# Softmax sums in smaller TensorE tiles, split by query halves, with a new instruction order (attention and a snake MLP on one core)

## The chip, the cores and the metric

The kernel runs on one core of a Trainium2 chip. The core has engines that each work through their own instruction queue in order: TensorE (PE: matmuls; PEld: its weight loads), VectorE (DVE), ScalarE (ACT), GpSimd (POOL) and SyncE (SP, which only issues transfers). They meet through semaphores. Operands lie in SBUF, matmul results in PSUM. The metric is the device time of the core in microseconds, from the first instruction to the last; lower is better.

## The reference

Attention with RMS-normalised queries and keys over 8 batches, 12 heads, 448 positions and head size 64, and then a two-layer product whose activation is `h + sin(alpha h)^2 / alpha`:

```python
def _attn_ref(q, k, v, g_q, g_k):          # q, k, v: (8, 12, 448, 64)
    q_n, k_n = (rmsnorm(q, g_q), rmsnorm(k, g_k))
    scores = np.matmul(q_n, k_n.transpose(0, 1, 3, 2)) / np.sqrt(q.shape[-1])
    attn = np.exp(scores - np.max(scores, axis=-1, keepdims=True))
    attn = attn / (np.sum(attn, axis=-1, keepdims=True) + 1e-09)
    return np.matmul(attn, v)

def _moe_ref(x, w_in, w_out, alpha):       # x: (3584, 768), d_ff 2048
    h = x @ w_in
    s = np.sin(alpha * h)
    g = h + s * s / (alpha + 1e-09)
    return g @ w_out
```

The rows of `x` are the positions of all batches, its columns the heads side by side. Inputs and output are float32. The kernel computes in bf16 on TensorE and leaves out the maximum before the exponential.

## The kernel before

Per batch, the 12 heads are three chunks of four heads: two head pairs `pp` by two halves `hi`. Each chunk is normalised, transposed, and multiplied to scores with the keys on the partitions, one tile of 64 keys per head at a time (seven tiles `j` make 448 keys). A score tile fills a PSUM pair of banks; ScalarE turns it into `expT`.

```python
    def scores(c, j, warm=0):

        sc = bank_pair("sc")
        for _ in range(warm):
            nc.tensor.matmul(sc[:, 0], blank[:, :P], blank, start=True, stop=True)
        for pp in range(2):
            for hi in range(2):
                qkt, r = qkT[2 * c + pp], slice(hi * 64, hi * 64 + 64)
                nc.tensor.matmul(sc[pp * 64:pp * 64 + 64, hi, :S], qkt[r, 1, j * REST:(j + 1) * REST], qkt[r, 0, :],
                                 start=True, stop=True)
        expT[c, j] = epool.tile([P, 2, S], BF16, tag="expT", name="expT")
        nc.scalar.activation(expT[c, j], sc[:, :, :S], ACT.Exp, scale=SCALE)
        give_back(sc)

    avs, recs = {}, {}
```

The sums over the keys come from a product with ones, so that each sum stands on all partitions of its head, where the product with the values stands too. `attend` does both. The first chunk of a batch ("ones 0", "values 0") uses 64x64 tiles: half `hi` of the heads on output partitions `hi * 64`, head pair `pp` in its own PSUM bank. The other two chunks together ("ones 1", and the low and high columns of the values) use 64x32 tiles in four strips of 32 partitions. Ln and Exp(-x) on ScalarE give the reciprocals `rec`, and VectorE multiplies the values with them into `xT`:

```python
    def attend(b, what, tiles=range(NJ)):

        kind, both = what.split()
        both = both == "1"
...
        last = 1 if pre else NJ - 1
        for j in tiles:
            for hi in range(2):
                for c in ((1, 2) if both else (0,)):
                    for pp in range(2):
                        r = slice(pp * 64, pp * 64 + 64)
                        o, k = (strip(c, pp, hi), c - 1) if both else (slice(hi * 64, hi * 64 + 64), pp)
                        d = slice(kind == "high", D, 2) if both and kind != "ones" else slice(D // 2 if both else D)
                        w = ones[r, d] if kind == "ones" else vb[b][r, 2 * c + hi, j, d]
                        x = pre.parts[j] if pre else expT[b * NC + c, j]
                        nc.tensor.matmul(av[o, k, :S], w, x[r, hi, :], start=(j == 0), stop=(j == last))
        if tiles[-1] < last:
            return
        if kind == "ones":
            rec = recs[both] = pre.t if pre else rpool.tile([P, 2, S], F32, tag="rec", name="rec")
            for k in ((0, 1), (1, 2)) if both and b == 0 else ((0, 2),):
                nc.scalar.activation(rec[:, slice(*k)], av[:, slice(*k), :S], ACT.Ln)
                nc.scalar.activation(rec[:, slice(*k)], rec[:, slice(*k)], ACT.Exp, scale=-1.0)
            give_back(avs.pop(what))
        else:
            if b not in xT:
                xT[b] = xpool.tile([P, KT, S], BF16, tag="xT", name="xT")
            first = 0 if not both else 2 if kind == "low" else 3
            for k in (slice(0, 1), slice(1, 2)) if both and b == 0 else (slice(0, 2),):
                kts = slice(first + k.start * (1 + both), first + (k.stop - 1) * (1 + both) + 1, 1 + both)
                nc.vector.tensor_mul(xT[b][:, kts, :], av[:, k, :S], recs[both][:, k])
            give_back(avs.pop(what))

```

(`pre` is not used by these plans: no batch adds tiles up beforehand.) Then come the first product (`hps`, 16 row tiles `m` of 128, over six row groups `kt` of the weights in the order 0, 1, 2, 4, 3, 5), the snake activation, and the second product, which is left over as filler work for the next batch's attention. Its pieces ("units") each hold a PSUM pair for 16 steps; a filler call does two steps, eight 64x64 matmuls:

```python
    def snake(b, ps, m):
        hps = ps[:, m % 2, :S]
        s1 = spool.tile([P, S], F32, tag="s1", name="s1")
        nc.scalar.activation(s1, hps, ACT.Sin, scale=alpha_sb[:, m, :])
        s2 = spool.tile([P, S], F32, tag="s2", name="s2")
        if m % 2 == 0:
            nc.gpsimd.tensor_mul(s2, s1, s1)
        else:
            nc.scalar.activation(s2, s1, ACT.Square)

        def finish():
            nc.vector.scalar_tensor_tensor(
                g_sb[:, m, (b % 2) * S:(b % 2 + 1) * S], s2, inv_alpha_sb[:, m, :], hps, op0=ALU.mult, op1=ALU.add)
            if m % 2:
                give_back(ps)
        return finish
...
                for r in range(2):
                    for o in range(2):
                        rs, os = slice(r * 64, r * 64 + 64), slice(o * 64, o * 64 + 64)
                        nc.tensor.matmul(st["ps"][os, r, :HALF], g_sb[rs, m, c0 + o * 64:c0 + o * 64 + 64],
                                         w_out_sb[rs, m, half * HALF:(half + 1) * HALF], start=(m == 0), stop=(m == MT - 1))
                if m == MT - 1:
                    ...
                    nc.vector.tensor_copy(osb[:, 0], st["ps"][:, 0, :HALF])
                    nc.vector.tensor_add(osb[:, 0], osb[:, 0], st["ps"][:, 1, :HALF])
                    give_back(st["ps"])
```

The order of all this is written out as plans: one for batch 0, one for batch 1, one for batches 2 to 7. In a plan `S` is a score tile (with a number: that many warming matmuls first), a number alone is so many filler calls on the current unit, `f` one on the next unit, `o` and `v` are tiles of the first chunk's sums and values, `x`, `y`, `z` those of the other chunks' sums, low and high values. `q`, `u`, `g`, `r`, `k`, `p`, `t` are the steps of the normalisation (square, reduce, gains, reciprocal root, scale, transpose on TensorE or by DMA) of a chunk; `l`, `V`, `W`, `O` load queries and keys, values, first and second weights; `D` lets GpSimd wait for a chunk's keys. The string of digits says which of the four PSUM pairs each taker gets; the dictionary says what goes beside the first product.

Of the kernel before, what the change touches and what calls it, by code (L numbers as in the profile page):

```python
# [17 lines left out]
try:  # L18
# [7 lines left out]
AX = mybir.AxisListType  # L26
ACT = mybir.ActivationFunctionType
# [3 lines left out]

STAGE_0 = (
    (
        "q000 u000 G q010 q011 u010 q001 u011 r01 u001 r00 g00 q11 q10 g01 k01 D1 k00 V00 L p012 p00 u10 "
        "V01 u11 W12 S2 S q20 r1 u20 g1 k11 l3 q21 k10 S2 l4 S S4 S W01 g2 S1 u21 p1 r2 k20 o7 S1 V02 S "
        "q30 k21 v7 u30 S S4 q31 D2 u31 S S1 W00 p2 r3 S3 g3 S S2 k31 S2 q40 D4 W02 S2 k30 q41 p3 S1 u40 "
        "W10 l5 W11 O01 q51 S x4 u41 y3 q50 S r4 z2 z2 x3 y4 g4 z1 z2 "
    ),
    "30123103213013230120310232103102310231302130213",
    {-1: 'u50 u51 g5', 1: 'k401 O00 l6', 2: 'k411', 3: 'O10', 4: 'k400', 5: 'k410', 7: 'O11', 8: 'p4 V12 l7 V10 V11'},  # L40
)
STAGE_1 = (
    (
        "2 q31 4 q40 S 2 u31 S 1 S 1 S r2 1 f q41 1 f 1 S S 1 f f k21 k20 1 S t2 2 S 2 S 1 u40 u41 1 q30 "
        "g3 S 2 f o2 u30 S r4 f 1 f 1 S 1 f o5 2 f r3 l5 2 f g4 f S 2 S 2 V11 S 1 S 2 k31 v1 k41 k30 k40 "
        "S v2 S v4 V12 S y1 S y1 S z3 x7 z3 q51 y5 l6 V10 z1 "
    ),
    "0212310313131230222101013032013001230123",
    {-1: 'l7 q50', 0: 'u51', 2: 'g5 t4', 4: 'u50', 8: 't3'},
)  # L50
STAGE_N = (
    (
        "1 r2 q31 q30 f 2 S V10 f 3 V11 f f k20 2 S 3 S 2 k21 S u31 q40 1 t2 1 g3 1 S 1 f u30 S 2 f S f S "
        "r3 q41 f f 1 l5 1 f S 4 u40 S S 5 S S u41 o7 v7 S S 5 S 2 q51 f S 2 S q50 k31 k30 2 S g4 1 u50 S "
        "2 r4 t3 1 S z3 x7 k40 y7 z1 z2 z1 "
    ),
    "01232302102020301301320321310130210231023",
    {-1: 'l6 u51 V12', 1: 'k41', 2: 't4 l7', 3: 'g5'},
)
LAST = "0123012"  # L60

# [7 lines left out]
def kernel(  # L69
# [23 lines left out]
    nc = tc.nc  # L93
    B, H, S, D = q.shape
# [8 lines left out]
    NJ = S // REST  # L103
    assert P == 2 * REST == 2 * D
    NC = NP // 2
# [28 lines left out]
    def bank_pair(name, dtype=F32):  # L134
        slot = int(upcoming.popleft())
        free_at.remove(slot)
        ps = psum.tile([P, 2, 2048 // mybir.dt.size(dtype)], dtype, tag=f"ps{slot}", name=name)
        slot_of[id(ps)] = slot
        return ps

    def give_back(ps):
        free_at.append(slot_of.pop(id(ps)))
# [3 lines left out]
    def strip(c, pp, hi):  # L146

        s = 2 * hi + (pp if c == 1 else 1 - pp)
        return slice(s * 32, s * 32 + 32)

    def load_qk(ci, k_queue=nc.sync):

        b, dp = ci // NC, ci % NC
        qk[ci] = inp.tile([P, 2, 2 * NJ, D], F32, tag="qk", name="qk")
        for which, src, queue in ((0, q, nc.sync), (1, k, k_queue)):
            heads = src[b].rearrange("(dp hi pp) (p j) d -> dp pp p hi (j d)", hi=2, pp=2, j=NJ)[dp]
            rows = qk[ci][:, which].rearrange("p (hi j) d -> p hi (j d)", hi=2)
            if ci == 0:
                continue
            if dp < 2:  # L160
                queue.dma_start(out=rows, in_=heads.rearrange("pp p hi x -> (pp p) hi x"))
            else:
                for pp in range(2):
                    queue.dma_start(out=rows[pp * 64:pp * 64 + 64], in_=heads[1 - pp])
        if ci == 0:
            for hi in range(2):
                for which, src, queue in ((0, q, nc.sync), (1, k, k_queue)):
                    heads = src[b].rearrange("(dp hi pp) (p j) d -> dp hi pp p (j d)", hi=2, pp=2, j=NJ)[dp, hi]
                    rows = qk[ci][:, which].rearrange("p (hi j) d -> p hi (j d)", hi=2)
                    queue.dma_start(out=rows[:, hi], in_=heads.rearrange("pp p x -> (pp p) x"))  # L170
                if hi == 0:
                    load_g()
# [17 lines left out]
    def load_g():  # L190
        for i, (src, queue) in enumerate(((g_q, nc.sync), (g_k, nc.scalar))):
            queue.dma_start(out=g_rows[:, i], in_=src.rearrange("(a d) -> a d", a=1))

    load_qk(0, nc.scalar)
    load_qk(1, nc.scalar)
    load_qk(2)
    nc.gpsimd.dma_start(out=small, in_=moe_alpha.rearrange("(mt p) -> mt p", p=P))
    nc.scalar.preload_act_table_set(EXP_LN)
# [2 lines left out]
    ones = const.tile([P, D], BF16)  # L201
# [58 lines left out]
    qkT, expT, xT = {}, {}, {}  # L260
# [125 lines left out]
# [6 lines that stand above are left out]
        if tiles[0] == 0:  # L392
            avs[what] = bank_pair("av")
        av = avs[what]
        pre = presums.get(b) if what == "ones 0" else None
        last = 1 if pre else NJ - 1
        for j in tiles:
            for hi in range(2):
                for c in ((1, 2) if both else (0,)):
                    for pp in range(2):  # L400
# [7 lines that stand above are left out]
            return  # L408
        if kind == "ones":
            rec = recs[both] = pre.t if pre else rpool.tile([P, 2, S], F32, tag="rec", name="rec")  # L410
            for k in ((0, 1), (1, 2)) if both and b == 0 else ((0, 2),):
                nc.scalar.activation(rec[:, slice(*k)], av[:, slice(*k), :S], ACT.Ln)
                nc.scalar.activation(rec[:, slice(*k)], rec[:, slice(*k)], ACT.Exp, scale=-1.0)  # L413
            give_back(avs.pop(what))
# [8 lines that stand above are left out]
# [185 lines left out]
    for b in range(B):  # L608
        plan, slots, h_plan = (STAGE_0, STAGE_1, STAGE_N)[min(b, 2)]
        if b:  # L610
            nc.scalar.preload_act_table_set(EXP_LN)
            fillers.extendleft(reversed(second_product(b - 1)))
        tiles = deque((b * NC + c, j) for c in range(NC) for j in range(NJ))
        upcoming.extend(slots)
        done = {what: 0 for what in STEPS}
        for x in tokens_of(plan):
            if x in "Ff":
                fill(x == "f")
            elif x[0] == "S":
                scores(*tiles.popleft(), int(x[1:] or 0))  # L620
            elif x[0] in STEPS:
                n = int(x[1:] or 1)
                attend(b, STEPS[x[0]], range(done[x[0]], done[x[0]] + n))
                done[x[0]] += n
            else:
                step(b, x)
        first_product(b, {i: [lambda t=t: step(b, t) for t in tasks.split()] for i, tasks in h_plan.items()})
        assert not upcoming and not tiles
# [32 lines left out]
```

## The time and profile before

The median of three runs is 417.75 us (417.33 to 418.62). The profiled execution spans 417.9 us.

| | busy us | share of the span |
|---|---|---|
| TensorE (PE) | 397.1 | 95% |
| ScalarE (ACT) | 317.4 | 76% |
| GpSimd (POOL) | 285.3 | 68% |
| VectorE (DVE) | 227.1 | 54% |

| group | count | busy us |
|---|---|---|
| first product, L449 | 768 matmuls | 146.8 |
| second product in quadrants, L528 | 3072 matmuls | 145.6 |
| exponentials, L361 | 168 | 144.9 |
| scores, L358 | 672 matmuls | 58.3 |
| sums and values, L406 | 1792 matmuls | 62.4 |

How to read it: busy times of one engine's groups overlap where matmuls of several tiles run side by side, so a group's busy time is the union of its records and not its share of the total. A matmul's own duration (349 ns for 448 columns) contains the passage through the array; the pace is read from the distance between the starts of groups. "Idle before" with a releaser says what an engine waited for. Idle time of an engine that does not set the pace costs nothing.

### The profile page before, as it was taken

How to read it: one execution, taken by the hardware profiler on the slowest of the kernel's cores; microseconds unless marked ns; L12 is line 12 of the kernel's file. 1: busy time of each engine (PE TensorE's matmuls, PEld its weight loads, DVE VectorE, ACT ScalarE, POOL GpSimd, SP SyncE). 2: the span in 40 equal slices, each digit the busy share in tenths (PEclk: the TensorE clock that was granted, in tenths of full speed). 3: DMA queues.
4: the chain of work that ended last, by engine and by line, in shares of the span. 5: the costliest groups of instructions: out<-in, count | busy, mean ns of one | idle time of the engine just before them, and what ended most of it. 6: DMA issues, size and time to landing. Idle time of an engine off the chain costs nothing.

```text
span 417.9 us, 14897 instructions
## 1 busy us (share of the span) xinstructions
PE 397.1 (95%) x6598; PEld 238.2 (57%) x6601; DVE 227.1 (54%) x339; ACT 317.4 (76%) x467; POOL 285.3 (68%) x270
## 2 busy tenths in 40 slices
PE   2797999889999999999999999999999999999996
PEld 2243558645666557655666456655576556665563
DVE  5786475426674565564575466655565464335511
ACT  4897789748889679877889688987889688886600
POOL 4999889966786879597796688597795784003300
PEclk9999999999999999999999999999999999999999
DMA  8999999798085744847374744736385521620022
GB/s 244 212 220 255 167 218 156 168 284 105 3 164 131 168 139 83 175 92 156 101 175 119 174 134 80 176 81 164 104 131 158 93 46 27 96 61 0 2 75 75
DMA packets 66788, 54.51 MB, mean 130 GB/s; under 512 B 38164, under 2 KB 62500, under 8 KB 66724
## 3 DMA queue, kind: packets, MB, share of 16 engines
q1 hardware_dynamic: 53250, 40.06, 37.8%
q0 software_dynamic: 12512, 11.81, 19.7%
q10 hardware_dynamic: 962, 1.70, 1.1%
q8 instruction: 51, 0.84, 0.8%
q14 instruction: 13, 0.11, 0.1%
HBM read 45.62 MB, written 11.01 MB: 136 GB/s over the span
## 4 chain that ended last, share of the span: by engine, by line
PE 86%; DMA 6%; POOL 4%; issue 2%; DVE 1%; ACTq 0%; SPq 0%; ACT 0%; DVEq 0%; POOLq 0%
PE hps L449 34%; PE ops L528 29%; PE av L406 11%; PE sc L358 6%; PE ops L509 5%; DMA w_in<-in_moe_w_in_dram 3%; DMA qk<-in_k_dram 2%; POOL sq L283 1%; DMA out_dram<-osb 1%; POOL qk L288 1%; POOL vb L182 0%; POOL vb L185 0%; SPq L499 0%; POOL w_in L244 0%; DVE osb L534 0%
## 5 line engine op out<-in xcount | busy, mean ns | idle before, releaser
L361 ACT ACTIVATE expT<-sc 128x896 bf16<-128x896 f32 x168 | 144.9, 914 | 16.9 <-PE sc L358 16.0
L449 PE MATMUL hps<-xT,w_in 128*128 128x448 bf16 x768 | 146.8, 353 | 2.1 <-DMA w_in<-in_moe_w_in_dram 2.1
L528 PE MATMUL ops<-w_out_sb,g_sb 64*64 64x384 bf16 x3072 | 145.6, 323 | 0.2 <-ACT expT L361 0.2
L435 DVE SCALAR_TENSOR_TENSOR g_sb<-s,inv_alpha_sb,hps 128x448 bf16<-128x448 f32 x128 | 80.8, 677 | 67.3 <-POOL s L430 66.9
L449 PEld LDWEIGHTS <-w_in 128*128 128x128 bf16 x768 | 74.4, 98 | 74.0 <-issue 3.0
L528 PEld LDWEIGHTS <-g_sb 64*64 64x64 bf16 x3072 | 91.3, 107 | 38.0 <-issue 2.7
L430 POOL TENSOR_TENSOR s<-s 128x448 f32<-128x448 f32 x64 | 59.5, 932 | 74.7 <-ACT s L427 50.2
L427 ACT ACTIVATE s<-hps,alpha_sb 128x448 f32<-128x448 f32 x128 | 74.4, 626 | 43.2 <-PE hps L449 40.4
L283 POOL TENSOR_TENSOR sq<-qk 128x896 f32<-128x896 f32 x44 | 73.3, 1682 | 26.1 <-DMA qk<-in_k_dram 21.1
L311 POOL TENSOR_TENSOR qkn<-qk,inv 128x448 bf16<-128x448 f32 x80 | 72.7, 938 | 2.5 <-ACT inv L302 2.0
L358 PE MATMUL sc<-qkT 64*64 64x448 bf16 x672 | 58.3, 356 | 3.6 <-DVE qkT L343 2.1
L534 DVE COPY osb<-ops 128x384 f32<-128x384 f32 x48 | 26.7, 557 | 51.3 <-PE ops L528 46.1
L288 POOL TENSOR_TENSOR qk<-qk,gg 128x896 f32<-128x896 f32 (+1 forms) x25 | 50.3, 2016 | 1.2 <-ACT g_sb L280 1.1
L292 DVE TENSOR_REDUCE ms<-sq 128x14 f32<-128x896 f32 x44 | 46.7, 1078 | 6.4 <-POOL sq L283 6.3
L421 DVE TENSOR_TENSOR xT<-av,rec 128x896 bf16<-128x896 f32 (+1 forms) x26 | 25.6, 1015 | 37.2 <-ACT rec L413 30.7
L406 PE MATMUL av<-expT,vb 64*32 64x448 bf16 (+1 forms) x1120 | 37.9, 350 | 2.7 <-issue 2.0
L432 ACT ACTIVATE s<-s 128x448 f32<-128x448 f32 x64 | 36.9, 577 | 3.0 <-DVE g_sb L435 0.2
L358 PEld LDWEIGHTS <-qkT 64*64 64x64 bf16 x672 | 20.7, 107 | 17.3 <-issue 7.9
L406 PEld LDWEIGHTS <-vb 64*32 64x32 bf16 (+1 forms) x1120 | 19.5, 95 | 16.7 <-issue 6.8
L535 DVE TENSOR_TENSOR osb<-osb,ops 128x384 f32<-128x384 f32 x48 | 26.6, 554 | 1.7
L406 PE MATMUL av<-expT,ones 64*32 64x448 bf16 (+1 forms) x672 | 24.5, 349 | 0.0
L509 PE MATMUL ops<-w_out_sb,g_sb 128*128 128x384 bf16 x128 | 21.0, 326 | 0.0
(46 smaller groups left out, 173.5 us busy)
## 6 DMA issues: line engine op xcount, KB each, us to landing
out_dram<-osb SPq DMA_DIRECT2D x39, 192.0 KB, 3.7
qk<-in_q_dram SPq DMA_DIRECT2D x15, 448.0 KB, 5.5
qk<-in_k_dram SPq DMA_DIRECT2D x14, 448.0 KB, 6.3
qk<-in_q_dram SPq DMA_DIRECT2D x18, 224.0 KB, 4.3
qk<-in_k_dram SPq DMA_DIRECT2D x16, 224.0 KB, 4.7
vb<-in_v_dram POOLq DMA_DIRECT2D x16, 224.0 KB, 4.4
w_out_sb<-in_moe_w_out_dram POOLq DMA_DIRECT2D x4, 768.0 KB, 7.7
out_dram<-osb SPq DMA_DIRECT2D x26, 96.0 KB, 3.4
```

Of the source, the lines that this page charges most:

```text
L283: nc.gpsimd.tensor_mul(st.sq[w], qk[ci][:, w], qk[ci][:, w])
L288: nc.gpsimd.tensor_mul(x, x, gg.to_broadcast([P, len(heads) * NJ, D]))
L292: nc.vector.reduce_sum(st.ms[:, w, rows], st.sq[w][:, rows], axis=AX.X)
L311: eng.tensor_mul(n[:, :, hi, :], x[:, hi], inv[:, hi].unsqueeze(2).to_broadcast([P, NJ, D]))
L358: nc.tensor.matmul(sc[pp * 64:pp * 64 + 64, hi, :S], qkt[r, 1, j * REST:(j + 1) * REST], qkt[r, 0, :], start=True, stop=True)
L361: nc.scalar.activation(expT[c, j], sc[:, :, :S], ACT.Exp, scale=SCALE)
L406: nc.tensor.matmul(av[o, k, :S], w, x[r, hi, :], start=(j == 0), stop=(j == last))
L427: nc.scalar.activation(s1, hps, ACT.Sin, scale=alpha_sb[:, m, :])
L430: nc.gpsimd.tensor_mul(s2, s1, s1)
L435: nc.vector.scalar_tensor_tensor(g_sb[:, m, (b % 2) * S:(b % 2 + 1) * S], s2, inv_alpha_sb[:, m, :], hps, op0=ALU.mult, op1=ALU.add)
L449: nc.tensor.matmul(ps[:, m % 2, :S], w_in_sb[m * 2 // MT][:, kt, m % (MT // 2) * P:(m % (MT // 2) + 1) * P], x[:, kt, :], start=(kt == ORD ...
L528: nc.tensor.matmul(st["ps"][os, r, :HALF], g_sb[rs, m, c0 + o * 64:c0 + o * 64 + 64], w_out_sb[rs, m, half * HALF:(half + 1) * HALF], star ...
```

## The change

For batches 1 to 7 the sums of the first chunk are no longer formed in 64x64 tiles. Each tile's 448 queries are cut in two halves `qh`, and each half is multiplied with only 32 columns of ones, so that the sums of query half `qh` of heads `hi` stand on the strip of 32 partitions `2 * hi + qh`. That makes eight 64x32 tiles of 224 columns where four 64x64 tiles of 448 columns were. It is meant to use TensorE for half as many columns. The product with the values still wants all 448 reciprocals on all 64 partitions of its head, so the missing half is brought over from the partner strip: VectorE "sums" over an axis of one element, reading 32 partitions and writing another 32. ScalarE takes Ln of half as many elements and writes Exp(-x) twice, once into the other half of the columns as the source of these moves.

The plans are all new, with the same number of score tiles, filler calls and warming matmuls (apart from one filler call of each plan that works on the current unit instead of the next). In batch 0 the sums stay as they were. The keys of the second chunk are loaded by SyncE's queue instead of ScalarE's. The diff:

```diff
--- before.py
+++ after.py
@@ -31,31 +31,31 @@
 
 STAGE_0 = (
     (
-        "q000 u000 G q010 q011 u010 q001 u011 r01 u001 r00 g00 q11 q10 g01 k01 D1 k00 V00 L p012 p00 u10 "
-        "V01 u11 W12 S2 S q20 r1 u20 g1 k11 l3 q21 k10 S2 l4 S S4 S W01 g2 S1 u21 p1 r2 k20 o7 S1 V02 S "
-        "q30 k21 v7 u30 S S4 q31 D2 u31 S S1 W00 p2 r3 S3 g3 S S2 k31 S2 q40 D4 W02 S2 k30 q41 p3 S1 u40 "
-        "W10 l5 W11 O01 q51 S x4 u41 y3 q50 S r4 z2 z2 x3 y4 g4 z1 z2 "
+        "q010 u010 G q000 q011 u011 q001 u000 r01 u001 g00 g01 r00 q10 D1 k01 k00 V02 W00 p012 q11 g1 W02 "
+        "u10 p00 q21 u11 r1 q20 k11 k10 S2 V00 g2 S1 l3 S S2 u21 S u20 S1 r2 W11 q30 L l4 p1 k20 k21 S2 "
+        "q31 S3 u30 S1 u31 S2 S S1 o1 S4 p2 r3 V01 S D2 g3 k31 W01 l5 o3 W10 o3 D4 W12 k30 S1 v7 S1 p3 "
+        "q40 q41 u40 S S2 S1 O01 q50 S1 S u41 x3 O00 y2 y4 x4 y1 z7 r4 g4 u50 q51 "
     ),
-    "30123103213013230120310232103102310231302130213",
-    {-1: 'u50 u51 g5', 1: 'k401 O00 l6', 2: 'k411', 3: 'O10', 4: 'k400', 5: 'k410', 7: 'O11', 8: 'p4 V12 l7 V10 V11'},
+    "12010210130112302302310203231023103210321032132",
+    {-1: 'O10 u51 k410 l6', 0: 'O11', 2: 'k411', 3: 'g5', 5: 'k401 k400', 6: 'V10', 8: 'p4 V12 V11 l7'},
 )
 STAGE_1 = (
     (
-        "2 q31 4 q40 S 2 u31 S 1 S 1 S r2 1 f q41 1 f 1 S S 1 f f k21 k20 1 S t2 2 S 2 S 1 u40 u41 1 q30 "
-        "g3 S 2 f o2 u30 S r4 f 1 f 1 S 1 f o5 2 f r3 l5 2 f g4 f S 2 S 2 V11 S 1 S 2 k31 v1 k41 k30 k40 "
-        "S v2 S v4 V12 S y1 S y1 S z3 x7 z3 q51 y5 l6 V10 z1 "
+        "1 q31 2 S 2 q30 2 f 2 r2 S 1 u31 S q41 2 S S 2 k20 f k21 f S t2 f 1 S u30 3 S 1 f S 1 q40 l5 g4 "
+        "1 g3 2 S f S 3 u41 1 u40 o6 V12 o1 v1 2 S 2 f r3 v4 S v2 1 k31 f S f S 1 S f 1 S 1 k30 1 t3 S "
+        "q50 2 S S z4 l6 S r4 x5 x1 z1 x1 y6 V11 y1 z1 z1 g5 k41 k40 "
     ),
-    "0212310313131230222101013032013001230123",
-    {-1: 'l7 q50', 0: 'u51', 2: 'g5 t4', 4: 'u50', 8: 't3'},
+    "0132102102023301312322121210213130123023",
+    {-1: 'l7 u50', 0: 't4 q51', 2: 'V10', 8: 'u51'},
 )
 STAGE_N = (
     (
-        "1 r2 q31 q30 f 2 S V10 f 3 V11 f f k20 2 S 3 S 2 k21 S u31 q40 1 t2 1 g3 1 S 1 f u30 S 2 f S f S "
-        "r3 q41 f f 1 l5 1 f S 4 u40 S S 5 S S u41 o7 v7 S S 5 S 2 q51 f S 2 S q50 k31 k30 2 S g4 1 u50 S "
-        "2 r4 t3 1 S z3 x7 k40 y7 z1 z2 z1 "
+        "f q40 f 1 f 2 q41 1 S 1 r2 5 f S f f S 2 S 1 u40 k20 1 k21 S 1 u41 1 S 2 S 1 q31 1 o7 1 f f 1 S "
+        "t2 f 1 r4 S 2 f 1 l5 q30 S 3 S 1 u31 1 S 2 u30 g3 V10 S 2 S S k41 3 S v6 r3 k30 S k31 v1 S 2 V12 "
+        "g4 2 S 2 S 2 q51 l6 S t3 z3 x7 y5 y2 z4 V11 "
     ),
-    "01232302102020301301320321310130210231023",
-    {-1: 'l6 u51 V12', 1: 'k41', 2: 't4 l7', 3: 'g5'},
+    "01223131310312323203013012301021310231023",
+    {-1: 'k40', 0: 't4', 2: 'q50', 3: 'u50', 4: 'u51 g5', 6: 'l7'},
 )
 LAST = "0123012"
 
@@ -192,7 +192,7 @@
             queue.dma_start(out=g_rows[:, i], in_=src.rearrange("(a d) -> a d", a=1))
 
     load_qk(0, nc.scalar)
-    load_qk(1, nc.scalar)
+    load_qk(1)
     load_qk(2)
     nc.gpsimd.dma_start(out=small, in_=moe_alpha.rearrange("(mt p) -> mt p", p=P))
     nc.scalar.preload_act_table_set(EXP_LN)
@@ -394,7 +394,16 @@
         av = avs[what]
         pre = presums.get(b) if what == "ones 0" else None
         last = 1 if pre else NJ - 1
+        halved = what == "ones 0" and b > 0
         for j in tiles:
+            if halved:
+                for hi in range(2):
+                    for qh in range(2):
+                        for pp in range(2):
+                            r, o = slice(pp * 64, pp * 64 + 64), slice((2 * hi + qh) * 32, (2 * hi + qh) * 32 + 32)
+                            nc.tensor.matmul(av[o, pp, :S // 2], ones[r, :D // 2], expT[b * NC, j][r, hi, qh * S // 2:(qh + 1) * S // 2],
+                                             start=(j == 0), stop=(j == NJ - 1))
+                continue
             for hi in range(2):
                 for c in ((1, 2) if both else (0,)):
                     for pp in range(2):
@@ -408,7 +417,16 @@
             return
         if kind == "ones":
             rec = recs[both] = pre.t if pre else rpool.tile([P, 2, S], F32, tag="rec", name="rec")
-            for k in ((0, 1), (1, 2)) if both and b == 0 else ((0, 2),):
+            if halved:
+                cols = [slice(0, S // 2), slice(S // 2, S)]
+                nc.scalar.activation(rec[:, :, cols[0]], av[:, :, cols[0]], ACT.Ln)
+                nc.scalar.activation(rec[:, :, cols[1]], rec[:, :, cols[0]], ACT.Exp, scale=-1.0)
+                nc.scalar.activation(rec[:, :, cols[0]], rec[:, :, cols[0]], ACT.Exp, scale=-1.0)
+                for hi in range(2):
+                    for qh in range(2):
+                        src, dst = (slice((2 * hi + x) * 32, (2 * hi + x) * 32 + 32) for x in (qh, 1 - qh))
+                        nc.vector.reduce_sum(rec[dst, :, cols[qh]], rec[src, :, cols[qh]].unsqueeze(3), axis=AX.X)
+            for k in () if halved else ((0, 1), (1, 2)) if both and b == 0 else ((0, 2),):
                 nc.scalar.activation(rec[:, slice(*k)], av[:, slice(*k), :S], ACT.Ln)
                 nc.scalar.activation(rec[:, slice(*k)], rec[:, slice(*k)], ACT.Exp, scale=-1.0)
             give_back(avs.pop(what))
```

## The prediction

> **What bounds the kernel now.** I read the page's busy shares first, then the busy time of each engine in windows cut where a batch's first product (line 449) starts, then TensorE's waits, then groups by line and shape, then TensorE in order of time.
>
> ```profile
> PE 397.1 (95%) x6598; PEld 238.2 (57%) x6601; DVE 227.1 (54%) x339; ACT 317.4 (76%) x467; POOL 285.3 (68%) x270
> ```
>
> ```profile
> 0.00:41.79 41.79, 28.99 (x459) 13.83 (x462) 29.62 (x51) 30.87 (x48) 34.86 (x41) 1.00 1.01 233
> 41.79:90.20 48.41, 44.82 (x805) 29.54 (x806) 23.18 (x37) 39.27 (x57) 44.87 (x45) 1.00 0.98 189
> 90.20:137.50 47.30, 47.30 (x853) 28.82 (x854) 27.76 (x41) 37.97 (x57) 32.16 (x28) 1.00 0.58 115
> 137.50:184.81 47.31, 47.31 (x855) 28.83 (x854) 27.09 (x40) 39.07 (x58) 37.35 (x34) 1.00 0.58 136
> ...
> 374.87:417.90 43.03, 39.07 (x225) 21.77 (x224) 16.18 (x23) 14.74 (x25) 7.46 (x8) 0.98 0.14 38
> ```
>
> After the length come busy PE, PEld, DVE, ACT, POOL, then the granted clock, DMA share and GB/s. There are three regimes. From 90 to 375 us TensorE is busy for all of each 47.3 us period: what leaves TensorE there leaves the total, and work on VectorE (27 of 47 us) is free unless it delays TensorE. Up to 90 us the DMA engines are full (1.01 and 0.98) and GpSimd nearly so (44.87 of 48.41); TensorE is idle 48.41 - 44.82 = 3.6 us in the second window. The last window has no attention in it.
>
> ```profile
> PE hps L449 <- DMA w_in<-in_moe_w_in_dram: 2.1, 1, 2.1
> PE av L406 <- issue: 2.0, 2, 1.6
> PE sc L358 <- DVE osb L535: 1.4, 1, 1.4
> ```
>
> The idle time that a better order could recover is small: 2.1 us for weights at 39.7 us, 1.4 us at 79 us for a PSUM pair that VectorE has not emptied, 1.6 us at 87.8 us with no releaser shown.
>
> ```profile
> L406 PE MATMUL av<-expT,ones 64*32 64x448 bf16 x448 | 12.3, 349 | 0.0
> L406 PE MATMUL av<-expT,ones 64*64 64x448 bf16 x224 | 12.2, 349 | 0.0
> L413 ACT ACTIVATE rec<-rec 128x448 f32<-128x448 f32 x2 | 1.2, 577 | 0.1
> L412 ACT ACTIVATE rec<-av 128x448 f32<-128x448 f32 x2 | 1.1, 534 | 0.1
> L292 DVE TENSOR_REDUCE ms<-g_sb 128x7 f32<-128x448 f32 x4 | 2.3, 612 | 3.5 <-ACT g_sb L280 3.5
> ```
>
> The second row is what is changed. Half the matmuls (224 against 448) take as long as the first row, because four 64x64 tiles stream at once and eight 64x32 tiles do too. In order of time:
>
> ```profile
> 83.13 0.38 PE L406 MATMUL av<-expT,vb 64*32 64x448 bf16 x8 [0.43 <-DVE osb L535]
> 83.45 0.38 PE L358 MATMUL sc<-qkT 64*64 64x448 bf16 x4
> 83.76 0.38 PE L406 MATMUL av<-expT,vb 64*32 64x448 bf16 x8
> ...
> 121.87 1.79 PE L528 MATMUL ops<-w_out_sb,g_sb 64*64 64x384 bf16 x40
> 123.50 0.55 PE L358 MATMUL sc<-qkT 64*64 64x448 bf16 x8
> 123.88 1.49 PE L406 MATMUL av<-expT,ones 64*64 64x448 bf16 x28
> 125.20 1.49 PE L406 MATMUL av<-expT,vb 64*64 64x448 bf16 x28
> ```
>
> From start to start the sums take 125.20 - 123.88 = 1.32 us, or 0.189 us for each of seven groups. A second-product group takes (123.50 - 121.87) / 10 = 0.163 us for 384 columns. So a column costs (189 - 163) / 64 = 0.41 ns, with some 3 ns per group. Where a 64x32 group and a 64x64 group alternate (83.13, 83.45, 83.76), they stand 0.31 to 0.32 us apart instead of 0.19: a change of tile shape costs some 0.12 us.
>
> **What the Trainium skill says.** "TensorEngine Tiling (Array Packing)", Key Properties: changing the tiling mode, not just the tile, drains TensorE. The trace agrees, with the 0.12 us above. "TensorE: Matmul & The Clock Gate", Measured speedup vs the span model: tiles in a pack are issued some 4 ns apart. In the trace the eight matmuls from 133.34 us on start 3 to 4 ns apart, so eight need about 28 ns of issue, below the 93 ns that 224 columns stream. The same page, Back-to-back issue gap, has a floor near 25 ns per matmul at small sizes; eight at 25 ns would be 200 ns. The trace speaks against it for separate tiles: a 64x32 pair already comes every 0.189 / 8 = 23.6 ns. The same page, LDWEIGHTS: a load costs its columns divided by 1.2 per ns, 27 ns for 32 columns; four such in each row half would be 107 ns, an estimate and slightly over the streaming time. No run yet has 64x32 tiles with fewer than 448 columns, so this is the open point of the arithmetic.
>
> **Part 1, the sums.** A group of 224 columns is 224 x 0.41 + 3 = 96 ns, or 107 if loads bind. Seven take 0.67 to 0.75 us instead of 1.32: 0.57 to 0.65 us less in each of batches 1 to 7. Before, the neighbours had the same shape; now, in each plan, they are 64x64 matmuls on both sides of one block of sums, so two drains are added, 0.24 us. Net: 0.4 us per batch on the engine that sets the end. Seven batches: **-2.8 us**.
>
> **Part 2, the reciprocals.** ScalarE had 0.92 + 0.95 = 1.87 us; now one Ln and two Exp over 448 elements, 0.53 + 2 x 0.58 = 1.69 us: 0.2 us less, on an engine with 9 us free per period. VectorE gains four sums of 448 elements each; the nearest row is the 0.61 us reduction, fewer partitions saving nothing: 2.45 us per batch, 17 us in all, beside TensorE. What counts is the delay. In the order for batches 2 to 7 the sums stand between the emptying of two second-product units. I lay the tokens end to end with the durations above: the sums end at 10.5 us, the next unit at 14.1 us, and its PSUM pair is wanted again at 16.1 us. The chain after the sums is 1.69 + 2.45 = 4.1 us, starting when ScalarE has finished the pending exponentials, so VectorE is free at 14.8 to 15.2 us, and two operations of 0.56 us empty the pair by 15.9 to 16.3. That is a stall of nothing to 0.2 us per batch; I take 0.1: **+0.7 us**. The values multiply waits for these reciprocals, but its matmuls come some 9 us later now, not at once.
>
> **Part 3, the order.** Batch 0: as much GpSimd work stands ahead of the last weight piece that the first product waits for (four squares, three folds, six weight and value issues), so that piece is issued near 30 us as now, and lands some 11 us later behind full DMA engines. It is now needed after 8 matmuls instead of 12, worth up to 0.7 us of loss, while two of the projections' pieces come earlier. I put batch 0 at 0. Batch 1: score tiles no longer alternate with 64x32 values near its end (twice two drains, some 0.5 us), and the late second-product units finish 1 to 1.6 us later in the token sum, which suits VectorE's wait for output buffers (the 1.4 us). ScalarE's exponentials and GpSimd's near-full load limit the rest. I take **-2.0 us** of the 3.6 us idle and the drains. Batches 2 to 7 and the end have nothing left for an order to recover.
>
> Sum: 417.75 - 2.8 + 0.7 - 2.0 = 413.65, say **413.6 us**.
>
> **Rivals.** (a) Issue or weight loads bind, and eight small pairs take as long as four large ones. Then the drains remain, 7 x 0.24 = +1.7 us, and with the order's gain the time is 417.4. The 3 to 4 ns starts speak against it, the load figure a little for it. (b) VectorE's 2.45 us become a wait: it stands in order behind ScalarE, and a PSUM pair comes back late. At 0.7 us per batch it eats the whole gain: 419 without the order's help, 417.5 with it. The thin slack in part 2 speaks for it; VectorE's 20 idle us per period against. (c) The first 90 us are bound by DMA whatever the order, so nothing comes of part 3: 415.6. The DMA share of 1.0 speaks for it. (d) The order removes most of the 3.6 and 2.1 us idle as well: 410.
>
> **Range and chances.** Part 1 is good to 0.5 us or so, part 2 to 2 us on the bad side, part 3 to 3 us either way. Joined, 409.8 to 418.2. Over 2% faster is below 409.4, for which everything must go right: 0.09. Over 2% slower is above 426.1, which needs a new stall of 1.5 us in every batch: 0.04. Within 2%: 0.87.
>
> **What would show it.** Right: the row of sums becomes 392 matmuls of 64x32 with 224 columns, from start to start 0.67 to 0.75 us for 56; TensorE's period from first product to first product falls to 46.8 to 47.1 us with no new wait; the one-element sums take some 0.6 us each; the first product of batch 2 starts near 88 us instead of 90.2. Wrong: 56 sums in 1.3 us (rival a); TensorE waiting for line 553 or for the reciprocals in every period (rival b); the second period's start still at 90 us (rival c).

## The result and the profile after

The changed kernel takes 413.78 us (median, 413.23 to 414.99) against 417.82 us for the kernel before on the same chip: a ratio of 0.9905, 95% interval 0.9879 to 0.9932. A second comparison, on another chip, gave 414.17 us and 0.9933 (0.9907 to 0.9959). The prediction was 413.6 us.

The busy line of the changed kernel's page:

```profile
PE 397.1 (96%) x6795; PEld 240.0 (58%) x6797; DVE 243.4 (59%) x367; ACT 315.9 (76%) x474; POOL 286.2 (69%) x270
```

TensorE's busy time is what it was, 397.1 us, although the sums stream half as many columns. The total hides the gain. From batch 1's first product to that of the last batch six periods later, TensorE is busy for 2.3 us less; first before and then after:

```profile
90.20:374.87 284.67, 284.24 (x5113) 173.06 (x5114) 158.10 (x231) 232.51 (x338) 198.08 (x179) 1.00 0.54 120
87.36:370.20 282.84, 281.92 (x5281) 176.57 (x5282) 171.47 (x255) 232.05 (x345) 201.42 (x183) 1.00 0.59 123
```

Ahead of batch 0's first product it is busy for 30.06 us instead of 26.54, in a stretch that is 40.00 us long instead of 37.20. VectorE has the 16 us more that the moves cost. The changed sums are one row now:

```profile
L404 PE MATMUL av<-expT,ones 64*32 64x224 bf16 x392 | 6.1, 258 | 0.0
```

The windows of the changed kernel, cut at the starts of the first products (columns as in the prediction):

```profile
40.00:87.36 47.36, 46.06 (x846) 28.11 (x846) 29.78 (x46) 40.12 (x63) 43.45 (x41) 1.00 0.99 181
87.36:134.28 46.92, 46.92 (x881) 29.39 (x882) 29.08 (x44) 38.85 (x59) 34.74 (x34) 1.00 0.61 134
134.28:182.51 48.23, 47.30 (x881) 29.58 (x882) 30.21 (x44) 39.77 (x59) 38.31 (x34) 1.00 0.64 134
```

The period fell from 47.31 to 46.92 us, with TensorE busy throughout as before: 0.39 us a batch. The third line is 1.31 us longer; it holds one passing stall of TensorE (0.78 us) with no releaser shown. The trace before had two smaller ones. A second profile of the changed kernel has only one period that is longer, by 0.26 us, so these stalls are not the kernel's own.

TensorE, then VectorE, then TensorE again in the changed kernel, in order of time, around the sums of batch 2:

```profile
114.70 0.82 PE L546 MATMUL ops<-w_out_sb,g_sb 64*64 64x384 bf16 x16
115.45 0.86 PE L404 MATMUL av<-expT,ones 64*32 64x224 bf16 x56
116.25 1.49 PE L546 MATMUL ops<-w_out_sb,g_sb 64*64 64x384 bf16 x32
```

```profile
118.19 2.48 DVE L428 TENSOR_REDUCE rec<-rec 32x448 f32<-32x448 f32 x4 [1.26 <-ACT rec L424]
120.70 0.56 DVE L552 COPY osb<-ops 128x384 f32<-128x384 f32 x1
121.29 0.55 DVE L553 TENSOR_TENSOR osb<-osb,ops 128x384 f32<-128x384 f32 x1
```

```profile
121.90 0.38 PE L358 MATMUL sc<-qkT 64*64 64x448 bf16 x4
```

Four groups of 0.163 us from 114.70 us end their stream at 115.35; the sums start at 115.45, so 0.10 us is a drain. To the next 64x64 matmul they take 0.80 us. Single records inside this block start 96 ns apart from group to group, and the last group stands 209 ns from its successor, 0.11 us too far: the drain on the way out. Seven groups of 96 ns and two drains make 0.88 us in place of 1.32; of these 0.44 us the period shows 0.39. The move of the reciprocals ends at 120.67, the second-product unit that waited behind it is emptied at 121.84, and the score tile that takes its PSUM pair starts 0.06 us later. Nothing waits here, and nothing is to spare. In batch 1 alone TensorE waits, 0.79 us at 78 us, for the product that follows the moves.

### The profile page after: what moved, and what is told of

Same layout as the page of the kernel before. It is cut to its first block, busy times and chain, and to the rows that moved or that the text cites. A ratio compares the mean times of both kernels' runs of the same rounds, so it can differ in the third digit from the quotient of the medians.

```text
span 413.2 us, 15331 instructions
## 1 busy us (share of the span) xinstructions
PE 397.1 (96%) x6795; PEld 240.0 (58%) x6797; DVE 243.4 (59%) x367; ACT 315.9 (76%) x474; POOL 286.2 (69%) x270
## 4 chain that ended last, share of the span: by engine, by line
PE 93%; ACT 2%; DVE 2%; DMA 1%; issue 1%; DVEq 0%
PE hps L467 35%; PE ops L546 29%; PE av L415 11%; PE sc L358 8%; PE ops L527 5%; PE sc L354 2%; PE av L404 1%; PE tp L336 1%; ACT expT L361 1%; DMA qk<-in_k_dram 1%; DVE ms L292 1%; DVE rec L428 1%; ACT g_sb L280 0%; DVE xT L439 0%; DVE qkT L343 0%
## 5 line engine op out<-in xcount | busy, mean ns | idle before, releaser
L546 PE MATMUL ops<-w_out_sb,g_sb 64*64 64x384 bf16 x3072 | 148.5, 323 | 0.0
L546 PEld LDWEIGHTS <-g_sb 64*64 64x64 bf16 x3072 | 92.4, 107 | 36.1 <-issue 3.2
L358 PE MATMUL sc<-qkT 64*64 64x448 bf16 x672 | 62.2, 364 | 2.3 <-DVE xT L439 0.8
L358 PEld LDWEIGHTS <-qkT 64*64 64x64 bf16 x672 | 22.5, 107 | 16.9 <-issue 10.3
L428 DVE TENSOR_REDUCE rec<-rec 32x448 f32<-32x448 f32 x28 | 17.1, 610 | 9.4 <-ACT rec L424 9.1
```

## The experiments

Theory: the sums give 0.39 us in each of seven batches, the moves nothing, and the order the rest. Rivals: the order gives it all; the sums give it in any order; the moves cost time that a shorter chain would give back.

**1. The new plans with the old sums, twice.** The branch that cuts the sums is switched off:

```diff
-        halved = what == "ones 0" and b > 0
+        halved = False
```

> The new plans with the sums of all batches in 64x64 tiles of 448 columns, as before. Theory A (the sums are worth what the trace of the changed kernel shows from period to period, 47.31 - 46.92 = 0.39 us a batch, and the rest is the order of batch 1): 413.8 + 7 x 0.39 = 416.5 us, period of batches 2 to 7 at 47.3 us. Rival B (the order does it all, the sums nothing): 413.8 us. Rival C (the new plans were fitted to the short sums and stall with the long ones): over 417.8 us.

> The new plans with the old sums once more, to narrow what the order is worth. Theory A (0.7 us): a ratio of 0.997 to 0.999. Rival B (2 us, as predicted): 0.995 or lower.

Measured: 416.22 us, ratio to before 0.9982 (0.9963 to 1.0000), and 415.98 us, 0.9964 (0.9946 to 0.9982). In the chain of the second run the first products of two batches stand 47.31 us apart again:

```profile
135.87 18.27 PE hps L467 x96
183.18 18.27 PE hps L467 x96
```

So the order by itself is worth about 0.27% (the mean of the two), 1.1 us, and the short sums the rest: the mean of the changed kernel's two ratios is 0.9919, so 0.54% or 2.3 us, beside 7 x 0.39 = 2.7 us from the periods. Rivals B and C of the first run fall. The second run lies between its two ranges. The 2.0 us that I had put down for the order would be a ratio of 0.9952: just inside the second run's interval, outside the first's and outside that of the mean of both, 0.9960 to 0.9986, which is 0.6 to 1.7 us.

**2. The old plans with the new sums.** The three plans and the load queue are those of before; the sums, reciprocals and moves are the changed ones.

> The plans and the load queue of before, with the new sums and moves. In the old plans the values follow the sums at once and their PSUM pair is wanted 3.2 us after the values end. Theory A (the chain of Ln, two Exp and four moves, some 4.1 us plus the product of 1.1 us, is too long for this place, and TensorE waits 1 to 2 us in each of batches 2 to 7; the new order is needed for the new sums): 415.1 + 6 x 1.0 to 1.7, so 421 to 425 us. Rival B (the moves are hidden in any order): 417.8 - 7 x 0.39 = 415.1 us.

Measured: 427.77 us, ratio 1.0263 (1.0239 to 1.0287), more than the 421 to 425 us that were expected. One of TensorE's waits and one period of this kernel:

```profile
PE sc L358 <- DVE xT L439: 8.2, 6, 1.5
```

```profile
188.12:236.81 48.69, 47.36 (x881) 29.81 (x882) 29.46 (x44) 38.79 (x59) 35.97 (x33) 1.00 0.54 127
```

That is one wait in each of batches 2 to 7, for the product of the values with the late reciprocals, which must empty their PSUM pair first. The periods are 48.7 us or more. In batch 1 there is another wait, of 3.18 us, for VectorE to empty a second-product unit, and after it the granted clock is 0.50 for 3.41 us. The same sums that gain 2.3 to 2.7 us in one order lose 11 in another: the new order is mainly what lets the sums pay.

**3. The moves twice, and not at all.**

```diff
-                        nc.vector.reduce_sum(rec[dst, :, cols[qh]], ...)
+                        for _ in range(2):
+                            nc.vector.reduce_sum(rec[dst, :, cols[qh]], ...)
```

> The changed kernel with each one-element sum on VectorE done twice (same values): 2.45 us more in each of batches 1 to 7, between the emptying of two second-product units. Theory A (the place has next to no slack: in the trace the pair is empty at 121.84 us and the score tile that takes it starts at 121.90): 1.5 to 2.4 us of waiting in each of batches 2 to 7, 413.8 + 9 to 15 us, so 423 to 429 us, and TensorE's waits name line 553. Rival B (VectorE is idle over a third of each period and takes it in): within 1 us of the changed kernel.

> The changed kernel without the four one-element sums: the partner strips keep the other half's reciprocals, so half of the first chunk's reciprocals in batches 1 to 7 are those of other queries; what is left out is the moving alone. Theory A (the moves end just in time and cost nothing): within 0.5 us of the changed kernel, period 46.92 us. Rival B (they cost the 0.1 us a batch of the prediction's second part, or more): 0.7 us or more faster, period 46.8 us or less.

Without the moves (the loop over strips is left out, so half of the first chunk's reciprocals belong to other queries): 414.49 us, ratio 0.9918 (0.9887 to 0.9949), beside 414.17 and 0.9933 for the changed kernel in the same comparison. Two first products in its chain:

```profile
229.04 18.27 PE hps L463 x96
275.95 18.27 PE hps L463 x96
```

46.91 us instead of 46.92: in batches 2 to 7 the moves cost nothing. In batch 1 the wait of 0.79 us is gone without them, but from the end of batch 0's first product to the start of batch 1's it takes 28.89 us instead of 29.09 and 29.13 (two profiles of the changed kernel), so they cost 0.2 us there at most. Doubled they cost far more than expected, 441.19 us, 1.0572 (1.0543 to 1.0601). TensorE's waits, TensorE in order of time and the windows of one period of that kernel:

```profile
PE sc L358 <- DVE osb L554: 14.4, 6, 2.4
```

```profile
173.96 0.82 PE L547 MATMUL ops<-w_out_sb,g_sb 64*64 64x384 bf16 x16
177.19 0.59 PE L358 MATMUL sc<-qkT 64*64 64x448 bf16 x4 [2.40 <-DVE osb L554]
177.51 1.54 PE L547 MATMUL ops<-w_out_sb,g_sb 64*64 64x384 bf16 x16
178.79 0.64 PE L358 MATMUL sc<-qkT 64*64 64x448 bf16 x4
```

```profile
140.00:177.10 37.10, 34.78 (x532) 20.75 (x525) 25.25 (x39) 28.17 (x44) 29.94 (x26) 1.00 0.69 113
177.10:180.51 3.41, 3.32 (x44) 2.36 (x47) 3.04 (x5) 1.83 (x2) 0.00 (x0) 0.51 0.60 154
```

The wait is the expected one, 2.40 us of the 2.48 that were added: there was no slack. But after it the granted clock is 0.51 for 3.41 us, and sixteen second-product matmuls take 1.28 us from start to start instead of 0.65. Half speed for 3.41 us is another 1.7 us, so the wait costs 4.1 us of the period's growth from 46.92 to 51.13. It does so in five batches of six. In batch 2 the same wait leaves the clock at 1.00 and costs only itself. Its wait, its period and the next one:

```profile
127.69 0.38 PE L358 MATMUL sc<-qkT 64*64 64x448 bf16 x4 [2.40 <-DVE osb L554]
```

```profile
90.57:140.07 49.50, 47.10 (x881) 29.86 (x882) 31.70 (x48) 39.43 (x60) 33.64 (x33) 1.00 0.55 121
140.07:191.20 51.13, 48.73 (x881) 30.52 (x882) 31.61 (x48) 39.00 (x59) 36.98 (x34) 0.97 0.68 124
```

In batch 1 a wait of 3.37 us, 0.79 in the changed kernel, halves the clock too. Six waits of 2.40 us, 2.58 us more in batch 1 and six times 1.7 us make 27.2 us; measured are 441.19 - 414.17 = 27.0. The Trainium skill, "TensorE: Matmul & The Clock Gate", The HAM clock gate, tells of such a gate, which halves the clock after an idle window of 3.4 us. The length of the half-speed stretch agrees; that 2.40 us of waiting were enough five times and not the sixth is this trace's word, not the page's. The waits of experiment 2, up to 1.5 us in its periods, left the clock at 1.00.

**4. One more change of tile shape.** In the plan of batches 2 to 7 the sums are asked for in two blocks, with one filler call between them:

```diff
- ... q31 1 o7 1 f f 1 S ...
+ ... q31 o3 1 o4 1 f f 1 S ...
```

> The changed kernel with the plan of batches 2 to 7 asking for three tiles of the sums, one filler call, then four tiles, instead of a filler call and then seven tiles: the same work with one more change to 64x32 tiles and back. Theory A (a change of shape drains, 0.10 us in and 0.11 us out in the trace): period 46.92 + 0.21 = 47.13 us, 6 x 0.21 = 1.3 us more in all. Rival B (the 0.11 us around the sums are pipeline ends that cost nothing when other work follows): period 46.92 us.

Measured: 415.27 us, ratio 0.9951 (0.9928 to 0.9974), 1.1 us over the changed kernel in the same comparison, with intervals that overlap; the period below is clear of them. TensorE in order of time, and one period:

```profile
113.15 0.50 PE L546 MATMUL ops<-w_out_sb,g_sb 64*64 64x384 bf16 x8
113.58 0.48 PE L404 MATMUL av<-expT,ones 64*32 64x224 bf16 x24
113.99 0.52 PE L546 MATMUL ops<-w_out_sb,g_sb 64*64 64x384 bf16 x8
114.44 0.58 PE L404 MATMUL av<-expT,ones 64*32 64x224 bf16 x32
```

```profile
227.59:274.76 47.17, 47.17 (x882) 29.19 (x882) 29.23 (x44) 38.79 (x59) 37.00 (x34) 1.00 0.63 135
```

A filler call takes 0.325 us between its like; here the next block starts 0.43 and 0.45 us after it, and three groups of sums (0.29 us) take 0.41. The period is 47.17 us, 0.25 us more. A drain is real, and some 0.12 us each way.

**5. The plans of batches 0 and 1 apart.** In the kernel before, plan 1 is replaced alone, plan 0 (with the load queue) alone; in the changed kernel plan 0 is put back. The load queue always goes with plan 0, so what it is worth was not tested.

> The kernel before, with only the plan of batch 1 replaced by the new one; old sums everywhere. Theory A (the gain that is not the sums comes from batch 1's plan: from the end of the first product of batch 0 to the start of batch 1's it falls from 32.35 to 29.09 us, of which 0.4 us are the sums): 417.8 - 2.9 = 414.9 us. Rival B (the stretch is short because of what the new plan of batch 0 leaves behind it, or its transfers): near 417.8 us.

> The kernel before with the plan of batch 0 and the load queue of the changed kernel; old sums, old plans else. (The run called before_newplan0 was the kernel before itself, handed over by mistake.) Theory A (the plans of batches 0 and 1 gain together only; batch 1's plan alone gave a ratio of 1.001, both 0.998): a ratio of 0.999 to 1.003. Rival B (batch 0's plan holds the whole of the order's gain): 0.998 or lower.

> The changed kernel with the plan of batch 0 and the load queue of before. Theory A (batch 0's plan brings nothing by itself: its first product ends at 57.85 us in the trace before and at 58.27 us in the changed one): 413.4 us, within 1 us. Rival B (the new plan of batch 0 relieves the transfers in batch 1, which are full there): the stretch after it is longer again and the time 415 to 416.5 us.

Measured, as ratios to the kernel before:

| plan 0 | plan 1 | sums | us | ratio |
|---|---|---|---|---|
| old | new | old | 417.39 | 1.0014 (0.9994 to 1.0033) |
| new | old | old | 418.31 | 1.0027 (1.0009 to 1.0045) |
| new | new | old | 416.22, 415.98 | 0.9982, 0.9964 |
| old | new | new | 414.87 | 0.9951 (0.9927 to 0.9974) |
| new | new | new | 413.78, 414.17 | 0.9905, 0.9933 |

Neither plan helps alone; plan 0 alone even costs about 1 us. Only the pair gains. Theory A of the first run falls, that of the second holds, and the third (414.87 us) lies between its two theories. In the last pair of rows plan 0 seems worth a little with the new sums, but the intervals touch. The first and fourth rows differ in the sums and in batches 2 to 7's plan: 0.63%, 2.6 us, measured in one comparison, again the 2.7 us of the sums, since that plan left the period at 47.31 us in experiment 1. By which transfer or wait the two depend on each other was not settled.

**6. The kernel before once more.**

> The kernel before, profiled once more. Its first profile came from a run of 419.68 us, 1.9 us over its median, while the changed kernel's profiles came from runs near its median. Theory A (the first profile shows an unlucky first 90 us, so the difference of the two traces there overstates the order's gain): batch 1's first product starts at 88 to 89 us instead of 90.13, and the periods of batches 2 to 7 are 47.31 us again. Rival B (the first 90 us are the same from run to run and the order gains 2.8 us there): 90.1 us again.

> The kernel before with the plan of batch 0 and the load queue of the changed kernel; old sums. With the three runs that have the other three pairs of plans it tells whether the plans of batches 0 and 1 gain together only. Theory A (they gain together: batch 1's plan alone gave a ratio of 1.001, both 0.998): a ratio of 0.999 to 1.003, no gain alone. Rival B (batch 0's plan holds the whole of the order's gain): 0.998 or lower.

Both runs are of the kernel before; the second does not have the plan that its expectation names. Measured: 416.97 us, 0.9999 (0.9976 to 1.0022), and 416.86 us, 1.0008 (0.9989 to 1.0027). In the chain of the first:

```profile
88.28 18.27 PE hps L449 x96
135.59 18.27 PE hps L449 x96
```

Batch 1's first product starts at 88.28 us, not at 90.20, and the period is the same 47.31 us. In the second run it starts at 87.28. The windows of these two that match the prediction's second one:

```profile
41.88:88.28 46.40, 44.63 (x805) 29.54 (x806) 23.97 (x37) 39.05 (x57) 44.01 (x43) 1.00 0.99 190
39.90:87.28 47.38, 44.83 (x805) 29.55 (x806) 25.12 (x39) 38.54 (x57) 45.89 (x45) 1.00 1.02 194
```

TensorE is idle there for 1.8 and 2.6 us, not for 3.6. The two runs of experiment 1 leave 1.0 and 0.8 us. So the first 90 us differ by up to 2.9 us between profiles of one kernel, not all taken on one chip; the profile from which I predicted came from a run of 419.68 us, 1.9 over its median.

## Why the prediction was right, point by point

- **Part 1, the sums (-2.8 us): right.** A group of 224 columns takes 96 ns, the value from two rows of the trace before, and not the 107 ns that the load figure would have made: the loads hide. Two drains of some 0.1 us were put at 0.24 us and measured 0.21 around the block, 0.25 when added once more. The period fell by 0.39 us, predicted 0.4. Rival (a) is out.
- **Part 2, the moves (+0.7 us): the place right, the size 0 to 0.2.** VectorE was expected free at 14.8 to 15.2 us after the first product, and was at 120.67 - 105.62 = 15.05; the pair was empty 0.06 us before it was wanted, so no stall came; in batch 1 the moves cost 0.2 us at most. Rival (b) is what happens a little beyond: 2.48 us more gave 2.40 us of waiting, and the old order gave a wait in each period. It did not happen in this order. Its two figures do not come out of its own sum: 7 x 0.7 us on top of 417.75 - 2.8 make 419.85 and, with the order, 417.85, not 419 and 417.5. Nothing rests on them.
- **Part 3, the order (-2.0 us): the term that was mis-sized; it measured -1.1 us** by experiment 1. The step that failed is "-2.0 us of the 3.6 us idle and the drains". I read those 3.6 us from one profile and took them as the kernel's own; two other profiles of that kernel have 1.8 and 2.6 (experiment 6), so part of them belonged to that one run, or to its chip. And I put batch 0 at nothing by itself: alone its plan costs 1 us, while plan 1 alone measured +0.6 us with zero inside its interval. Rival (c), nothing from the order, is as far from the measured 1.1 us as part 3; rival (d), 410 us, is out. That the piece of weights would be waited for after 8 matmuls did not come true either: in the changed kernel the first product of batch 0 starts at 40.0 us instead of 37.2 and runs its 18.27 us without a wait.
- **A sign that could not decide.** The first product at 90.20 us is that of batch 1, counted from 0, and not of batch 2. It was to start near 88 us, and it does (87.36, and 87.11 in the second profile). But the kernel before has 88.28 and 87.28 in its other two profiles, so this start by itself tells nothing of the order.
- **The sum.** -2.7, 0 and -1.1 make -3.8 us, against -4.0 us in the first comparison and -3.0 in the second. The closeness of 413.6 to 413.78 is partly two errors that cancel: 0.7 us too much for the moves, 0.9 too much for the order.

## What to carry to other kernels

Where an engine is busy for a whole period, count stream time from start to start, not busy time, and a saving of some tenths of a microsecond a period arrives in full, provided that the work moved to another engine ends before the buffer behind it is wanted; so change the order with the work, and look for that buffer's next taker. Before pricing idle time as recoverable, see whether a second profile of the same kernel has it. A small packed matmul should stand beside others of its tile shape: each change of shape takes a tenth of a microsecond.

## What the runs showed of the hardware that was not expected

With the moves doubled, a wait of 2.40 us on TensorE was followed by 3.41 us at half the granted clock in five batches of six, and cost 4.1 us there; in the sixth it cost only itself, and the waits of 1.5 us in the old order left the clock at 1.00. A possible reason comes out of the same trace. Its six half-speed stretches begin at 81.56, 177.14, 228.34, 279.54, 330.74 and 381.94 us, which are 28, 15, 15, 15 and 15 steps of 3.413 us apart. Fifteen steps before 177.14 is 125.94, and this instant cuts the wait that left the clock alone (125.28 to 127.69) into 0.66 and 1.75 us. In the other five batches 2.3 us of waiting or more lie between two such instants. So idle time seems to be judged in fixed stretches of 3.41 us; this is read from one run and was not tested.

Eight 64x32 matmuls of 224 columns, each with its own weight load, sustain one per 12 ns (96 / 8) when they go to eight different tiles. The floor near 25 ns that the Trainium skill, "TensorE: Matmul & The Clock Gate", gives under Back-to-back issue gap does not hold for such packs.
